# Other places for the weight clamps, both first M in one run, and one batch's state scores moved, in a block-recurrent attention with a gelu MLP behind it

## The chip, the cores and the metric

The kernel runs on one core of a Trainium2 chip. The metric is the time of one execution on the device, in microseconds (us); lower is better. Five runs of the kernel before the change gave a median of 696.96 us.

The engines have short names here: PE is the tensor engine (matmuls; PEld its weight loads), DVE the vector engine, ACT the scalar engine, SP the engine whose queue issues the DMAs. Each engine works through its own instructions in the order in which the kernel emits them. Matmuls write to PSUM, which is used here as eight banks of 128x512 floats.

## The reference

There are two parts. The first is attention between a sequence `x` (8 batches, 8 heads, 512 tokens, 64 wide) and a small state (32 rows per head). The second is a feed-forward layer on the result: 4352 tokens, 512 wide, 2048 hidden, with a gelu in its sigmoid form.

```python
scores = scale * np.matmul(x, state.transpose(0, 1, 3, 2))
a = softmax(scores)                      # over the 32 state rows
xread = np.matmul(a, state)
scores2 = scale * np.matmul(state, x.transpose(0, 1, 3, 2))
a2 = softmax(scores2)                    # over the 512 tokens
sread = np.matmul(a2, x)
out = np.concatenate([xread, sread], axis=2)
...
h = x @ w_in
g = h * (1.0 / (1.0 + np.exp(-1.702 * h)))
return g @ w_out
```

Here `softmax` stands for the lines that subtract the maximum, take the exponential and divide by the sum plus 1e-9. Everything is float32, but the weights `w_in` and `w_out` come as 64-bit floats and are turned into 32-bit floats on the chip.

## The kernel before, in words

**Weights.** The two weight matrices are read in 32 pieces, 16 of `w_in` (four chunks `c` of 512 hidden columns, four row blocks each, so pieces 0 to 3 belong to chunk 0) and 16 of `w_out`. A piece is loaded raw by SP (512 KB, line 199) and then rounded from 64-bit words to float32. The steps of one piece are, on DVE, a mask of the exponent bits (`mask`, line 221), on ACT two Relu passes that clamp the exponent and turn it into a power of two (`round_a`, lines 232 and 233; the pair is called a clamp here), and on DVE again four steps in `fraction` and `round_b`: the mantissa's upper bits (line 239), the sign into the power (line 250), the lower bits (line 253), and the product (line 257). Line 250 needs the clamp. Pieces 18 and 19 are clamped on DVE instead.

`powers_to(n)` emits mask and clamp of all pieces below `n` that have not had them. `round_to(n, ahead)` emits the rounding of all pieces below `n`; within the rounding of piece `i`, after line 250, it asks for the clamps of the pieces up to `i + ahead`, so `ahead` says how far the clamps run in front. `AHEAD` is 3. The masks and powers lie in four buffers, used in turn.

**Attention and the first product.** For batch `b` and chunk `c`, `att_M(b, c)` multiplies the state by the weights of the chunk (M, 8 matmuls in two passes each, line 375), and copies the two results out of PSUM on ACT (line 482). `up_x(b, f)` multiplies M by the transposed attention `aT` (2 matmuls in two passes each, line 553) and applies the gelu on ACT as it leaves PSUM (line 556). So no hidden value of a batch can be made before its M's copy. Batches 0 and 1 run through this by hand, in the order written in the kernel; batches 2 to 7 and the state rows follow through a general path with Strassen products.

The attention of batches 0 and 1 goes in these steps: `xT_chunk` transposes a quarter of x on PE (line 318) and copies it on ACT (line 319); `x_scores` makes its scores (line 325); `head_max`, `head_sub` (lines 338, 342, DVE), `head_exp` (line 346, ACT) and `head_norm` (lines 352 to 358, DVE) make the softmax; `head_back` transposes it into `aT` in two halves (`g`, line 367 on PE, line 368 the copy on ACT). `att_scores(b)` makes the other scores, state by x (line 375 as well), read only much later by `att_s_max` and `att_s_exp`. `keep_warm(n)` emits `n` matmuls of zeros that nobody reads.

**PSUM.** Four banks `bank_o` have fixed names; the last two of them are `held`, which take batch 0's scores first and batch 1's state scores later. Two banks of the pool `psH` rotate under the tag "h" (batch 1's scores, called `apart`, then the `up_x`), and two of the pool `psA` under the tag "att" (transposes and M). A bank can be written again when its last reader is done.

**Down products.** From about 79 us the down product of batch 0 runs in eight pairs (line 1402, `pair`), each after the rounding of two `w_out` pieces and after sums that DVE makes (line 1332). Batch 1's down product is `strassen_two` with `key == 1`: P1 and P2 by `product`, then P5 and others by `strassen_low`, which uses three banks x, y, z (line 696 is its matmul). Its beginning is

```python
product(x, a11, b11, True)
nc.scalar.copy(y, x)
at(1)
product(z, s1, t1, True)
nc.scalar.copy(c22, z)
at(2)
product(y, s2, t2)
```

Right before P5, P2 fills `bank_o[1]`, which is also the `o` that P5 is given, and the line `tt(osb, bank(1), k1)` reads it on DVE (line 752 is that helper).

Of the kernel before, what the change touches and what calls it, by code (L numbers as in the profile page):

```python
# [10 lines left out]
FP32 = mybir.dt.float32  # L11
# [9 lines left out]
def kernel(  # L21
# [30 lines left out]
    nc = tc.nc  # L52

    B, H, S, D = x.shape
# [3 lines left out]
    P = 128  # L58
    NPR = P // Ns
    NG = H // NPR  # L60
    NF = DF // P
    SCH = S // P
    ST = S + Ns
    FC = 512
# [17 lines left out]
    apool = ctx.enter_context(tc.tile_pool(name="apool", bufs=1))  # L82
# [10 lines left out]
    def att_ps(shape, name):  # L93
        return psA.tile(shape, FP32, tag="att", name=name)

    ident = konst.tile([P, P], FP32, name="ident")
# [18 lines left out]
    low = konst.tile([P, 6, S], FP32, name="low")  # L115
# [13 lines left out]
    def keep_warm(n, bank=None):  # L129
        ps = psH.tile([P, FC], FP32, tag="h", name="warm") if bank is None else bank  # L130
        for _ in range(n):
            nc.tensor.matmul(ps, zeros[:, :P], zeros, start=True, stop=True)
# [49 lines left out]
    AHEAD = 3  # L182
# [33 lines left out]
    def mask(i):  # L216

        _, hi = words(i)
        sc = low[:, 2 + i % (AHEAD + 1)].bitcast(I32)
        power[i] = sc  # L220
        nc.vector.tensor_scalar(sc, hi, 0x7FF00000, None, ALU.bitwise_and)  # L221
# [37 lines left out]
    done = {"load": 0, "a": 0, "b": 0, "credit": 0.0}  # L259
# [11 lines left out]
    def powers_to(n):  # L271
        while done["a"] < min(n, len(PIECES)):
            load_weights(done["a"] + 1)
            round_a(done["a"])
            done["a"] += 1

    def round_to(n, ahead=AHEAD):

        nin = NFC * NPR
        while done["b"] < min(n, len(PIECES)):  # L280
            i = done["b"]
            powers_to(i + 1)
            round_b(i, min(i + 1 + ahead, i + 3 if i > nin + 3 else i + 2 if i >= nin else nin), i >= nin or i + 1 < nin and (i + 1 < n or i >= NPR))
            done["b"] += 1
            while done["b"] > NPR and done["load"] < len(PIECES) and before(done["load"]) < done["b"]:
                load_weights(done["load"] + 1)
# [25 lines left out]
    def xT_chunk(b, c):  # L312

        if c == 0:
            A[b]["xT"] = apool.tile([P, NPR, S], FP32, tag="xT", name=f"xT_{b}")
        ps = att_ps([P, NPR, P], f"xT_{b}_{c}")
        for j in range(NPR):
            nc.tensor.transpose(ps[:, j], x_heads(b, c, j), ident)
        nc.scalar.copy(A[b]["xT"][:, :, P * c : P * (c + 1)], ps)

    def x_scores(b, c, banks):

        ps = banks[c // 2].rearrange("p (c g j n) -> p c g j n", c=2, g=NG, j=NPR)[:, c % 2]
        for j in range(NPR):
            nc.tensor.matmul(ps[:, :, j], A[b]["xT"][:, j, P * c : P * (c + 1)], pairs[:, j], start=True, stop=True)
# [22 lines left out]
    def head_norm(b):  # L348

        t = A[b]["e1"]  # L350
        sm = apool.tile([P, NS1], FP32, tag="sm", name=f"sm_{b}")
        nc.vector.reduce_sum(out=sm, in_=t.rearrange("p c g j n -> p (c g j) n"), axis=AX.X)
        nc.vector.tensor_scalar(sm, sm, eps, None, ALU.add)
        nc.vector.reciprocal(out=sm, in_=sm)
        sm = sm.rearrange("p (c g j) -> p c g j", c=SCH, g=NG)
        for g in range(NG):
            e = t[:, :, g]
            nc.vector.tensor_tensor(out=e, in0=e, in1=sm[:, :, g].to_broadcast((P, SCH, NPR, Ns)), op=ALU.mult)

    def head_back(b):  # L360

        a = A[b]
        a["aT"] = low[:, :NG] if b == 1 else apool.tile([P, NG, S], FP32, tag="aT", name=f"aT_{b}")
        for g in range(NG):
            ps = att_ps([P, SCH, P], f"aT_{b}_{g}")
            for c in range(SCH):
                nc.tensor.transpose(ps[:, c], a["e1"][:, c, g].rearrange("p j n -> p (j n)"), ident)
            nc.scalar.copy(a["aT"][:, g], ps.rearrange("p c q -> p (c q)"))

    def by_state(b, ps, rhs):  # L370

# [5 lines left out]
    def att_scores(b):  # L377
        a = A[b]
        a["s"] = bank_o[:NG] if b == 0 else bank_o[NG:]
        by_state(b, a["s"], lambda rows, j: a["xT"][rows, j])  # L380
# [89 lines left out]
    def att_M(b, c, spare=False, banks=None):  # L470

        m = mpool.tile([P, NG, FC], FP32, tag=f"M{turns['M'] % NFC if b < 2 else c}", name=f"M_{b}_{c}")
        turns["M"] += 1
        A[b]["M", c] = m
        name = f"M_{b}_{c}_"
        ps = banks or [
            psH.tile([P, FC], FP32, tag="h", name=name + str(g)) if spare else att_ps([P, FC], name + str(g)) for g in range(NG)
        ]
        by_state(b, ps, lambda rows, j: w_in[c][rows, j])
        for w in (slice(0, P), slice(P, FC)) if (b, c) == (0, 0) else (slice(0, FC),):  # L480
            for g in range(NG):
                nc.scalar.copy(m[:, g, w], ps[g][:, w])  # L482


    squares = dram.tile([SCH, Ns, NG, NPR, P], FP32, name="squares")
# [72 lines left out]
    def up_x(b, f, spare=False, bank=None):  # L558
        c, o = divmod(P * f, FC)
        m = A[b]["M", c]  # L560
        up(b, f, S, [m[:, g, o : o + P] for g in range(NG)], [A[b]["aT"][:, g] for g in range(NG)], spare, bank)

    S1, S2 = (later[:, 4 * i : 4 * i + 4].rearrange("p f n -> p (f n)").rearrange("p (f t) -> p f t", f=HF) for i in range(2))
# [79 lines left out]
    low_a, low_b = ([low[:, 3 * i + k].rearrange("p (f n) -> p f n", f=QF) for k in range(3)] for i in range(2))  # L643
# [44 lines left out]
    def strassen_low(left, right, bank, R, at):  # L688

        b11, t3, b21, b22, t1, t2, t4 = right  # L690
        a11, a12, a21, a22, s1, s2, s4 = left
        x, y, z = (v[:, :P] for v in bank)

        def product(ps, lhs, rhs, first=False):
            for f in range(QF):
                nc.tensor.matmul(  # L696
                    ps, lhs[f], rhs[:, f], start=(first and f == 0), stop=(f == QF - 1), skip_group_check=True
                )

        def add(out, x0, x1):  # L700
            nc.vector.tensor_tensor(out=out, in0=x0, in1=x1, op=ALU.add)

        c11, c12, c21, c22 = (R[:, i, P * k : P * (k + 1)] for i in range(2) for k in range(2))
# [7 lines that stand above are left out]
        nc.scalar.copy(c12, y)  # L711
        at(3)
        product(x, a12, b21)
        nc.scalar.copy(c11, x)
        at(4)
        product(y, a21, t3)
        add(c22, y, c22)
        at(5)
        product(z, s4, b22)
        add(c12, z, c12)  # L720
        at(6)
        product(y, a22, t4)
        nc.scalar.copy(c21, y)
        at(7)

    def strassen_two(key, dst, hooks, a4):

        B11, B21, B22 = w_out[:, :HF, :HN], w_out[:, HF:, :HN], w_out[:, HF:, HN:]
        g = [G[key, u] for u in range(HF)]
# [57 lines left out]
        def left_of(s, *rooms):  # L787
            z = [[s[:, QF * k + f, P * i : P * (i + 1)] for f in range(QF)] for i in range(2) for k in range(2)]
            return *z, *(blocks(v) for v in rooms)
# [42 lines left out]
        else:  # L832

            m = [mpool.tile([P, NG, FC], FP32, tag=f"M{i}", name="spare_M") for i in range(2)]
# [10 lines left out]
            o, h0, h1 = low_banks()  # L845
# [39 lines left out]
            hook(f"P5.{i}")  # L885

        b11, t3, b21, b22 = halves_of(T1)
        strassen_low(left_of(S1, *r), (b11, t3, b21, b22, *low_b), [h0, h1, o], p5, at)
        low_load(6, 1)
        hook("P5")  # L890
        o, h0, h1 = low_banks()
# [335 lines left out]
    mask(3)  # L1227
    xT_chunk(1, 2)
    x_scores(1, 1, apart)
    keep_warm(2, held[0])  # L1230
    xT_chunk(1, 3)
    x_scores(1, 2, apart)
    powers_to(4)
    head_norm(0)
    x_scores(1, 3, apart)
    head_back(0)
    keep_warm(4, held[0])
    round_to(NPR, 0)
    att_M(0, 0)
    powers_to(NPR + 1)  # L1240
    for i in range(2):
        head_max(1, i, apart)
    for i in range(2):
        head_sub(1, i, apart)
    head_exp(1)
    up_x(0, 0, bank=held[0])
    up_x(0, 1, bank=held[1])
    att_M(1, 0)
    round_to(NPR + 1, 0)
    mask(NPR + 1)  # L1250
    mask(NPR + 2)
    head_norm(1)
    up_x(0, 2)
    powers_to(NPR + 2)
    up_x(0, 3)
    att_scores(1)
    head_back(1)
    powers_to(NPR + 3)

    def turn(b, c, then, n=()):  # L1260

        for i in range(nper):
            if i == nper - 1 and then:
                att_M(*then)
            up_x(b, nper * c + i)
            if i < len(n):
                rounds(n[i])

    for i in range(nper):
        up_x(1, i)  # L1270
        if i + 1 < nper:
            round_to(done["b"] + 1, 2)
    att_M(0, 1)
    turn(0, 1, (1, 1), [1, 1, 1])
    round_to(3 * NPR)
    turn(1, 1, (0, 2), [1, 1])
# [310 lines left out]
```

## Time and profile before

| | |
|---|---|
| median of 5 runs | 696.96 us (696.46 to 697.17) |
| the profiled execution | 696.47 us |
| its span in the profile | 694.7 us |
| PE busy | 682.6 us, 98% of the span |
| DVE busy | 560.5 us, 81% |
| ACT busy | 324.3 us, 47% |
| granted PE clock | 0.999 |

The profile is one execution. Its span runs from the first to the last instruction that the profile records; the execution's own time is 1.77 us longer. Busy times are averages over stages that differ: between 37 and 46 us ACT is busy 8.55 of 9 us, between 90 and 130 us 15.53 of 40. A matmul's recorded duration overlaps the next one's, so a row of matmuls is best timed from start to start. "Idle before" an instruction is ascribed to what released it, as the semaphores let one infer.

### The profile page before, as it was taken

To read this page: it belongs to the slowest core of one execution; us is meant where nothing else is said; L and a number is where in the kernel's file an instruction comes from. 1 tells how busy PE (TensorE), PEld (TensorE's weight loads), DVE (VectorE), ACT (ScalarE), POOL (GpSimd) and SP (SyncE) were. 2 spreads that over 40 slices of the span, in tenths; PEclk is the share of its full clock that TensorE was granted. 3 is DMA by queue.
4 is the path that set the end of the run, shared out by engine and by line. 5 is a ranking of instruction groups with operands and counts; after the bars stand their busy time and mean duration, and the time that the engine had idled before them with its cause. 6 is when DMAs were issued, how large, how long until landed. Compare 5 with 4: busy or idle time off the path is not lost.

```text
span 694.7 us, 13670 instructions
## 1 busy us (share of the span) xinstructions
PE 682.6 (98%) x5378; PEld 583.1 (84%) x5378; DVE 560.5 (81%) x1074; ACT 324.3 (47%) x714; POOL 1.0 (0%) x9
## 2 busy tenths in 40 slices
PE   7999999999999999999999999999999999999996
PEld 4533587778998899889988999989988998999995
DVE  5889998999999888788969796988788895886540
ACT  5788844224337523753355435643375236421410
POOL 0000000000000000000000000000000000000000
PEclk9999999999999999999999999999999999999999
DMA  9911337056533564346541755176424740251001
GB/s 237 374 63 61 122 121 167 21 196 189 177 84 119 170 191 143 64 132 189 150 96 48 226 168 117 24 185 202 121 46 138 213 138 16 76 165 46 5 1 30
DMA packets 106320, 87.41 MB, mean 126 GB/s; under 512 B 64784, under 2 KB 85776, under 8 KB 106256
## 3 DMA queue, kind: packets, MB, share of 16 engines
q1 hardware_dynamic: 106256, 86.53, 43.4%
q8 instruction: 43, 0.70, 0.4%
q14 instruction: 21, 0.17, 0.1%
HBM read 68.94 MB, written 17.56 MB: 125 GB/s over the span
## 4 chain that ended last, share of the span: by engine, by line
PE 94%; DMA 2%; ACT 2%; SPq 1%; issue 0%; DVE 0%; DVEq 0%
PE low L696 28%; PE o L1106 15%; PE o L696 15%; PE upx L1106 6%; PE h L553 5%; PE M L375 4%; PE o L1402 4%; PE down L1402 3%; PE o L595 2%; PE upw L1106 2%; PE down_up L553 2%; PE o L745 1%; PE sr L524 1%; PE o L375 1%; PE upx_sr L1106 1%; DMA out_dram<-osb_sr 1%
## 5 line engine op out<-in xcount | busy, mean ns | idle before, releaser
L696 PE MATMUL low<-w_out,g_room 128*128 128x128 f32 x416 | 54.3, 276 | 0.0
L696 PEld LDWEIGHTS low<-w_out,g_room 128*128 128x128 f32 x416 | 50.5, 192 | 4.5 <-issue 4.2
L1106 PE MATMUL o<-ta,M 128*128 128x256 f32 x192 | 49.9, 382 | 0.0
L1106 PE MATMUL upx<-aT,M 128*128 128x256 f32 x192 | 49.3, 379 | 0.0
L696 PE MATMUL low<-low,g_room 128*128 128x128 f32 x336 | 43.3, 275 | 0.0
L1106 PEld LDWEIGHTS o<-ta,M 128*128 128x128 f32 x192 | 35.5, 190 | 5.9 <-ACT g_room L1152 1.6
L696 PEld LDWEIGHTS low<-low,g_room 128*128 128x128 f32 x336 | 40.3, 192 | 0.0
L1106 PEld LDWEIGHTS upx<-aT,M 128*128 128x128 f32 x192 | 36.0, 190 | 4.7
L482 ACT COPY M<-M 128x512 f32<-128x512 f32 (+2 forms) x61 | 30.9, 581 | 17.2 <-PE M L375 17.1
L1112 ACT ACTIVATE g_room<-o 128x512 f32<-128x512 f32 (+1 forms) x56 | 31.3, 560 | 10.4 <-PE o L1106 10.4
L696 PE MATMUL low<-sums,later 128*128 128x128 f32 x280 | 35.8, 275 | 0.0
L696 PEld LDWEIGHTS low<-sums,later 128*128 128x128 f32 x280 | 33.6, 192 | 0.1
L375 PE MATMUL M<-w_in,stT 64*32 64x512 f32 x472 | 33.0, 595 | 0.0
L752 DVE TENSOR_TENSOR g_room<-g_room 128x512 f32<-128x512 f32 x48 | 31.7, 685 | 0.2
L1106 PE MATMUL o<-ta,ms 128*128 128x256 f32 x120 | 30.8, 379 | 0.0
L1152 ACT COPY g_room<-o 128x512 f32<-128x512 f32 (+1 forms) x28 | 15.5, 555 | 25.4 <-PE o L1106 25.4
L1112 ACT ACTIVATE g_room<-g_room 128x512 f32<-128x512 f32 (+1 forms) x28 | 16.8, 600 | 20.8 <-DVE g_room L1115 20.8
L553 PE MATMUL h<-aT,M 128*128 128x512 f32 x56 | 25.3, 600 | 0.8 <-ACT M L482 0.8
L1106 PEld LDWEIGHTS o<-ta,ms 128*128 128x128 f32 x120 | 22.8, 190 | 3.1
L1106 PE MATMUL o<-aT,m 128*128 128x256 f32 x96 | 24.6, 379 | 0.0
L232 ACT ACTIVATE low<-low,edge 128x512 f32<-128x512 int32 x30 | 21.5, 718 | 4.8 <-DVE low L221 4.8
L696 PEld LDWEIGHTS o<-w_out,g_room 128*128 128x128 f32 x160 | 19.4, 192 | 5.0 <-issue 5.0
(293 smaller groups left out, 1627.5 us busy)
## 6 DMA issues: line engine op xcount, KB each, us to landing
low<-low SPq DMA_DIRECT2D x108, 256.0 KB, 2.7
low<-low SPq DMA_DIRECT2D x11, 768.0 KB, 4.4
later<-in_moe_w_out_dram SPq DMA_DIRECT2D x16, 512.0 KB, 3.4
w_out<-in_moe_w_in_dram SPq DMA_DIRECT2D x12, 512.0 KB, 5.2
xsq<-in_x_dram SPq DMA_DIRECT2D x96, 64.0 KB, 2.5
xn<-in_x_dram SPq DMA_DIRECT2D x12, 512.0 KB, 4.3
out_dram<-osb SPq DMA_DIRECT2D x15, 256.0 KB, 2.2
out_dram<-later SPq DMA_DIRECT2D x14, 256.0 KB, 2.1
```

The costliest lines, as they stand in the source:

```text
L232: nc.scalar.activation(out=sc.bitcast(FP32), in_=sc, func=AF.Relu, bias=edge[0], scale=-8.0)
L375: nc.tensor.matmul(ps[g][st], A[b]["stT"][rows, st], rhs(rows, j), start=True, stop=True)
L482: nc.scalar.copy(m[:, g, w], ps[g][:, w])
L524: nc.tensor.matmul(ps[st, g], e, v, start=(c == 0), stop=(c == SCH - 1),)
L553: nc.tensor.matmul(hps, lhs[i], rhs[i], start=(i == 0), stop=(i == n - 1))
L595: nc.tensor.matmul(ps[:, r], lhs[f][:, P * r : P * (r + 1)], rhs[:, f], start=(first and r == 0 and f == 0), stop=(f == HF - 1), skip_grou ...
L696: nc.tensor.matmul(ps, lhs[f], rhs[:, f], start=(first and f == 0), stop=(f == QF - 1), skip_group_check=True)
L752: nc.vector.tensor_tensor(out=out, in0=x0, in1=x1, op=op)
L1106: nc.tensor.matmul(ps[:, k], lhs[i][:, o : o + P], rhs[i], start=(first and k == 0 and i == 0), stop=(i == n - 1), skip_group_check=True,)
L1112: nc.scalar.activation(out=dst, in_=src, func=AF.Gelu_apprx_sigmoid)
L1152: nc.scalar.copy(c12, Y(u))
L1402: nc.tensor.matmul(ps7[name][:, HN * r : HN * (r + 1)], lhs[:, P * r : P * (r + 1)], rhs, start=(i == 0 and r == 0), stop=(i == HF - 1), s ...
```

## The change

The order of the work on batches 0 and 1 between about 19 and 52 us is written differently:

- The clamp of piece 3 is asked for ahead of the last x transposes of batch 1, no longer behind them.
- `head_back` takes its half `g` as an argument. Batch 0's halves stand between the score chunks of batch 1, batch 1's directly behind `up_x(0, 2)`.
- Three warming matmuls instead of four before the first M.
- The clamp of piece 4 is asked for within the rounding of piece 3; masks 5 and 6 come before batch 1's `head_max`.
- M(1, 0) follows M(0, 0) on PE and goes to the held banks; `up_x(0, 0)` and `up_x(0, 1)` go to the att banks instead of the held ones, and `up_x(1, 0)` and `up_x(1, 1)` to the held ones. The clamp of piece 5 stands before `up_x(0, 0)`, that of piece 6 behind the two halves of `head_back(1)`.
- The copies of M(0, 0) are two whole ones, no longer four parts.
- From piece 6 on, `round_to` runs three pieces ahead instead of two, so that the clamps of pieces 9 and 10 come one `up_x` earlier.
- `att_scores(1)` stands behind M(0, 1) instead of before `head_back(1)`.
- In batch 1's P5 the banks y and z are exchanged.

```diff
-    def head_back(b):
+    def head_back(b, g):
...
-        for g in range(NG):
-            ps = att_ps([P, SCH, P], f"aT_{b}_{g}")
...
@@ att_M
-        for w in (slice(0, P), slice(P, FC)) if (b, c) == (0, 0) else (slice(0, FC),):
-            for g in range(NG):
-                nc.scalar.copy(m[:, g, w], ps[g][:, w])
+        for g in range(NG):
+            nc.scalar.copy(m[:, g], ps[g])
@@ strassen_two
-        strassen_low(left_of(S1, *r), (b11, t3, b21, b22, *low_b), [h0, h1, o], p5, at)
+        strassen_low(left_of(S1, *r), (b11, t3, b21, b22, *low_b), [h0, o, h1] if key == 1 else [h0, h1, o], p5, at)
@@ the order written by hand
     x_scores(1, 1, apart)
+    powers_to(4)
     keep_warm(2, held[0])
     xT_chunk(1, 3)
+    head_norm(0)
+    head_back(0, 0)
     x_scores(1, 2, apart)
-    powers_to(4)
-    head_norm(0)
+    head_back(0, 1)
     x_scores(1, 3, apart)
-    head_back(0)
-    keep_warm(4, held[0])
-    round_to(NPR, 0)
+    keep_warm(3, held[0])
+    round_to(NPR, 1)
     att_M(0, 0)
-    powers_to(NPR + 1)
+    mask(NPR + 1)
+    mask(NPR + 2)
     for i in range(2):
         head_max(1, i, apart)
     for i in range(2):
         head_sub(1, i, apart)
     head_exp(1)
-    up_x(0, 0, bank=held[0])
-    up_x(0, 1, bank=held[1])
-    att_M(1, 0)
+    att_M(1, 0, banks=held)
+    powers_to(NPR + 2)
+    up_x(0, 0, True)
+    up_x(0, 1, True)
     round_to(NPR + 1, 0)
-    mask(NPR + 1)
-    mask(NPR + 2)
     head_norm(1)
     up_x(0, 2)
-    powers_to(NPR + 2)
+    for g in range(NG):
+        head_back(1, g)
+    powers_to(NPR + 3)
     up_x(0, 3)
-    att_scores(1)
-    head_back(1)
-    powers_to(NPR + 3)
...
     for i in range(nper):
-        up_x(1, i)
+        up_x(1, i, bank=held[i] if i < 2 else None)
         if i + 1 < nper:
-            round_to(done["b"] + 1, 2)
+            round_to(done["b"] + 1, 2 if i == 0 else AHEAD)
     att_M(0, 1)
+    att_scores(1)
     turn(0, 1, (1, 1), [1, 1, 1])
```

More of the change, by code (lines that the diff above doesn't have):

```diff
@@ L358, in head_norm @@
             nc.vector.tensor_tensor(out=e, in0=e, in1=sm[:, :, g].to_broadcast((P, SCH, NPR, Ns)), op=ALU.mult)
-    def head_back(b):
+    def head_back(b, g):
         a = A[b]
-        a["aT"] = low[:, :NG] if b == 1 else apool.tile([P, NG, S], FP32, tag="aT", name=f"aT_{b}")
-        for g in range(NG):
-            ps = att_ps([P, SCH, P], f"aT_{b}_{g}")
-            for c in range(SCH):
-                nc.tensor.transpose(ps[:, c], a["e1"][:, c, g].rearrange("p j n -> p (j n)"), ident)
-            nc.scalar.copy(a["aT"][:, g], ps.rearrange("p c q -> p (c q)"))
+        if g == 0:
+            a["aT"] = low[:, :NG] if b == 1 else apool.tile([P, NG, S], FP32, tag="aT", name=f"aT_{b}")
+        ps = att_ps([P, SCH, P], f"aT_{b}_{g}")
+        for c in range(SCH):
+            nc.tensor.transpose(ps[:, c], a["e1"][:, c, g].rearrange("p j n -> p (j n)"), ident)
+        nc.scalar.copy(a["aT"][:, g], ps.rearrange("p c q -> p (c q)"))
     def by_state(b, ps, rhs):
```

## The prediction, made before the changed kernel was run

> **What bounds the kernel now.** I read the page's busy shares and its chain first.
>
> ```profile
> PE 682.6 (98%) x5378; PEld 583.1 (84%) x5378; DVE 560.5 (81%) x1074; ACT 324.3 (47%) x714; POOL 1.0 (0%) x9
> ...
> PE 94%; DMA 2%; ACT 2%; SPq 1%; issue 0%; DVE 0%; DVEq 0%
> ```
>
> TensorE (PE) carries 94% of the chain, so an edit saves time only where PE stands still or does work that is not needed. The list of what PE waited for (us in total, times, longest) has these that the diff touches:
>
> ```profile
> PE h L553 <- ACT M L482: 2.0, 2, 1.2
> ...
> PE o L553 <- ACT M L482: 0.3, 1, 0.3
> PE o L696 <- DVE osb L752: 0.3, 1, 0.3
> ```
>
> Line 482 is the copy of an M out of PSUM, line 752 the DVE addition into osb in batch 1. The chain from 17 to 64 us, in order of time (start, us, what), shows how such a wait comes about:
>
> ```profile
> 24.54 1.68 PE M L375 x16
> ...
> 45.44 0.57 ACT M L482
> ...
> 50.68 0.72 ACT low L233
> 51.41 0.49 ACT g_room L556
> 51.89 0.62 ACT low L232
> ...
> 53.74 0.62 ACT low L232
> ...
> 54.38 0.72 ACT low L233
> 55.11 0.48 ACT M L482
> ...
> 55.63 5.42 PE h L553 x12
> ```
>
> Three things are to be seen. M of (batch 0, chunk 0) takes 1.68 us at 24.54, where the others take 1.02: its last quarter waits for piece 3, rounded on DVE until 25.06. At 45.44 PE waits for the copy of M(0,1), which the next matmul needs at once. From 48 to 55.6 the chain runs on ACT: gelu, clamp (L232, L233), gelu, clamp, and M(1,1)'s copy behind them, while PE stands 1.49 us (54.14 to 55.63). The busy time by stretch agrees (PE, PEld, DVE, ACT, POOL; the last numbers are granted clock, DMA share, GB/s):
>
> ```profile
> 25.00:37.00 12.00, 11.56 (x72) 4.23 (x60) 10.81 (x22) 9.72 (x18) 0.00 (x0) 1.00 0.78 313
> 37.00:46.00 9.00, 8.15 (x32) 3.14 (x32) 7.75 (x17) 8.55 (x16) 0.00 (x0) 1.00 0.00 0
> 46.00:56.00 10.00, 8.72 (x33) 3.35 (x34) 9.28 (x20) 8.29 (x16) 0.00 (x0) 1.00 0.55 172
> 56.00:64.00 8.00, 8.00 (x33) 3.13 (x32) 7.96 (x16) 5.87 (x11) 0.00 (x0) 1.00 0.12 47
> ```
>
> PE is idle 0.85 and 1.28 us of the second and third stretch, with ACT at 8.55 of 9 and 8.29 of 10; from 56 us on PE is full.
>
> **Prices.** A clamp costs ACT 1.37 us, a gelu 0.48, start to start:
>
> ```profile
> 49.94 0.71 ACT L232 ACTIVATE low<-low,edge 128x512 f32<-128x512 int32 x1
> 50.68 0.72 ACT L233 ACTIVATE low<-low,edge 128x512 int32<-128x512 f32 x1
> 51.31 0.58 ACT L556 ACTIVATE g_room<-h 128x512 f32<-128x512 f32 x1
> 51.79 0.71 ACT L232 ACTIVATE low<-low,edge 128x512 f32<-128x512 int32 x1
> ```
>
> From further timeline rows. ACT: copy of an M or an aT half 0.47 to 0.48; head_exp and the table load after it
>
> ```profile
> 28.67 1.04 ACT L346 ACTIVATE e<-e 128x1024 f32<-128x1024 f32 x1
> 29.73 1.28 ACT L556 ACT_TABLE_LOAD   x1
> 31.03 1.08 ACT L556 ACTIVATE g_room<-o 128x512 f32<-128x512 f32 x2
> ```
>
> 1.06 and 1.30. PE: an up_x 1.72, its gelu can start 2.02 after its start (37.15 to 39.17); an M 1.02, copies can start 1.20 after its start (60.98 to 62.18) and the next up_x 0.63 after the copy's start (45.42 to 46.05); half a head_back 0.43, its copy 0.69 after its start (35.82, 36.51); a chunk of scores 0.86, a warming matmul 0.215. DVE: first step of a rounding (L250) 0.61, mask and fraction 0.34 each, the other two 0.60.
>
> **The first part, 20 to 37 us.** Up to 20.8 only ACT differs: clamp 3 now stands ahead of the last xT copy, at 19.82, and ends at 21.28, not 23.01. DVE, which sat 1.01 us for it, does L250 of piece 3 at 21.97 instead of 23.04; mask 4 is put in between (the one piece asked for ahead), so piece 3 is done at 24.2, not 25.06. PE: half of head_back at 21.10 (DVE's first product ends 21.05), scores, the other half, scores, three warming matmuls instead of four, M(0,0) from 24.40 to 25.42 without its 0.66 wait, and M(1,0), now into the held banks, to 26.44. The M(0,0) copies in two runs instead of four make the first take 0.58 instead of 0.26, but M(1,0) lies over that: copies at 25.60 and 26.07, up_x(0,0) at 26.5, as before, with 1.02 of M already done. Clamp 4 sits in ACT's gap at 23.55.
>
> Masks 5 and 6 (0.34 each) now stand ahead of head_max, which starts at 24.8 (before 25.32); head_sub ends at 27.27 (27.79). ACT from there: head_exp 27.31, M(1,0) copies 28.37 and 28.84, clamp 5 29.31, table load 30.68, gelus (0,0) to (0,2) at 31.98, 32.46, 32.94. So the change adds a wait: up_x(0,0) and (0,1) now use the att banks, and head_back(1) needs them next. PE is done with up_x(0,2) at 31.75, stands until 32.60 (end of the first gelu, 0.58, plus 0.04), and ends head_back(1) at 33.5; all of PE's queue stands behind it. DVE has those inputs at 32.2 and is not the last. aT copies 33.42 and 33.9, clamp 6 34.37, gelu(0,3) 35.74. On PE up_x(0,3) ends at 35.35 and up_x(1,0) starts, 1.80 before its 37.15; batch 1's state scores (1.02) are still owed, so 0.78 is gained.
>
> A rule of the Trainium skill speaks against this place: ScalarE: Activation LUTs, What ACT_TABLE_LOAD costs, has each switch of set cost a drain beside the load, about 2.66 us in all. The rows here have the gelu 1.30 after the load's start; by the page's figure gelu(0,0) would come 1.36 later and this stage's final gain would be near 0.7 instead of 2.03.
>
> **The second part, 37 to 56 us.** ACT in the new order: gelu(1,0) 37.37, clamp 7, gelu(1,1) 39.22, clamps 8 and 9 (one more than before), gelu(1,2) 42.44, clamp 10, gelu(1,3) 44.29, M(0,1) copies 44.77. PE ends the four up_x at 42.25, M(0,1) at 43.27 and the state scores, now here, at 44.29; up_x(0,4) waits for the copy until 45.40 (before 46.05). So the scores cost nothing here, but the clamps pulled ahead delay the copy by 1.4, and PE stands 1.1. Then one clamp, not two, lies between gelu(0,4) and gelu(0,5): gelu(0,4) 47.42, clamp 11, gelu 49.27, clamp 12, gelu 51.12, clamp 13, M(1,1) copy 52.97, up_x(1,4) at 53.60 instead of 55.63: 2.03 us. PE waits there only 0.4. DVE keeps up: L250 of pieces 6 and 7 wait for their clamps until 35.9 and 39.2, piece 7 is done at 41.8 (M(0,1) needs it at 42.9), piece 15 at 60.7 against 63.8.
>
> What hides the rest: after 56 us the order is unchanged. DVE is 97% busy there, and must stay ahead of PE. Its closest result is the t_room sum ending 86.18 for a matmul at 86.75, 0.57; but DVE enters the stage 3.0 us earlier, PE 2.03. The rounding that waited 2.35 us for a load at 122.08 ends at 126.5, its matmul starts 128.73; that load is queued on SP behind x loads issued as DVE frees the raw pieces, so it moves too, and if it didn't, 2.19 covers 2.03. SP's order is unchanged.
>
> **The third part, batch 1's P5.**
>
> ```profile
> 164.54 1.05 PE L696 MATMUL low<-sums,later 128*128 128x128 f32 x8
> 165.16 0.69 DVE L752 TENSOR_TENSOR osb<-o,g_room 128x512 f32<-128x512 f32 x1 [0.59 <-ACT e L414]
> ...
> 165.90 1.16 PE L696 MATMUL o<-low,spare_M 128*128 128x128 f32 x8 [0.31 <-DVE osb L752]
> ```
>
> PE has the second product ready at 165.43 (164.54 and 8 instructions of 0.89 together) but its bank is the one osb is read from, until 165.85: 0.47 lost. With the two banks swapped the second product goes to h1, free since 162.3; ACT's copy into o takes over the wait, 165.90 to 166.2, and the third product is due at 166.32. So 0.47 goes; what is late next is a DVE sum ending 181.51 for a matmul at 182.09, 0.53. Ends: nothing, if the copy is later by 0.5, and 0.47.
>
> **Sum.** 2.03 + 0.47 = 2.50, off this execution's 696.47 (span 694.7, 1.77 around it): 693.97. The median of the five runs is 0.49 above this execution, so 694.5.
>
> Unknown prices. Masks 5 and 6 need weight pieces that before touched only at 30.0 and 30.95. Piece 4 landed 4.9 us after its issue, at 20.7; the furthest row is 11.3, of a piece issued at 20.88 into a full queue. At the 0.52 MB a piece and 400 GB/s of that stretch, piece 6 lands at 23.3, over 1 us before mask 6: nothing, nearest to the 4.9 row; the other end is rival three. Should head_back's first half wait for both DVE products, PE is 0.64 late at 24, inside its 0.85 wait for the bank.
>
> **Rivals.** One, ACT pays back: the pulled clamps fill ACT's queue without emptying it later, so up_x(1,4) follows up_x(0,4) at the old distance of 9.58. Then only 46.05 - 45.40 = 0.65 stays, plus 0.47: 695.8. For it: ACT is 8.55 of 9 busy. Against: the chain above counts two clamps there and the new order one.
>
> Two, DVE does not follow: if its 3 us are lost on the way (it waits for ACT's exps at 76.8 and for loads), the gain is capped by the 0.57 at 86.75, plus 0.47: 695.9. Against: what it waits for moves with PE.
>
> Three, slower: piece 6 lands by the 11.3 row, at 28.3, and mask 6, ahead of head_max on DVE, holds DVE until then instead of 24.46. The whole ACT chain from head_exp is 3.8 later, and 2.50 saved becomes 1.3 lost: 698.3. It decides from 2.5 us of delay, a landing after 27. Against: the piece issued two before it took 4.9.
>
> That the bank swap only moves the wait is the lower end of part three: 694.9.
>
> **Chances.** Forecast 0.70 (its own range 693.4 to 695.4: 0.7 either way on ACT's chain, whose two new waits of 0.85 and 1.1 can shrink or grow, with 0.35 between runs downward, or with half of P5's 0.47 upward), rivals one and two together 0.20 (695.6 to 696.6), three 0.07, no change for other reasons 0.03. Eight in ten lie from 693.4 to 696.3. A measurement here tells about 0.2%, 1.4 us, from no change: faster by more 0.74 (the forecast and an edge of the rivals), within 0.19, slower 0.07.
>
> **What would show it.** Right: M(0,0) takes 1.02; piece 3's L250 near 22; head_back(1) waits near 0.85 for a gelu; up_x(0,4) waits about 1.1 for M's copy; one clamp between the gelus of up_x(0,4) to (0,6); up_x(1,4) near 53.6; P5's second product 0.89 after the first. Wrong: DVE idle ahead of mask 4, 5 or 6 for a DMA; a gap of 2.7 between table load and gelu; up_x(0,4) later than 46; PE waiting for DVE from 79 to 147.

## The result, and the profile after

| | before | after |
|---|---|---|
| median of the runs on the same chips | 696.68 us (47 runs) | 694.50 us (26 runs) |
| the profiled execution | 696.47 us | 694.47 us |
| its span | 694.7 us | 692.7 us |

After to before is 0.9967, 95% interval 0.9960 to 0.9974: the changed kernel is 2.2 us faster, and the forecast was 694.5. In some executions of these kernels the granted PE clock falls to 0.50 near 20 us and they take some microseconds longer; where runs with a low mean clock weigh on a median, those with 0.998 or more are given beside it.

The page's line of PE and its chain by engine, after:

```profile
PE 682.1 (98%) x5377; PEld 583.3 (84%) x5377; DVE 560.7 (81%) x1074; ACT 324.0 (47%) x712; POOL 1.0 (0%) x9
...
PE 92%; SPq 2%; DMA 2%; ACT 2%; DVE 1%; issue 0%; DVEq 0%
```

PE does the same products and one warming matmul less. It is busy 0.5 us less (the row of M(0,0), which before held a wait for piece 3, is 1.09 long instead of 1.70), and the other 1.5 of the 2 us came out of its idle time. The list of PE's waits after (us in total, times, longest):

```profile
PE aT L367 <- ACT g_room L555: 1.1, 1, 1.1
PE h L552 <- ACT M L481: 1.1, 1, 1.1
```

Before there were two waits for M's copy, 2.0 in all, 0.3 for M(0,0), 0.3 for osb and 0.2 for a copy of aT. After there is one for M's copy, ahead of `up_x(0,4)`, the new one of `head_back(1)` for the bank that the first gelu must free, and 0.2 ahead of `head_back(0)`. The chain from 17 to 62 us (start, us, what) shows the same in order:

```profile
17.42 7.47 DMA w_out<-in_moe_w_in_dram
...
24.92 0.48 DVE low L221
25.40 1.20 DVE mx L338 x2
...
27.82 1.06 ACT e L346
...
31.24 1.28 ACT L555
...
32.53 0.61 ACT g_room L555
...
33.18 1.14 PE aT L367 x8
...
45.31 0.48 ACT M L481
...
45.84 5.42 PE h L552 x12
51.26 1.02 PE M L375 x16
52.28 7.19 PE h L552 x16
```

It begins with a weight load that lands 7.47 us after its issue, on which mask 6 waits at the head of `head_max`. It then goes through the softmax and ACT (head_exp, M(1,0) copies, clamp 5, table load, first gelu). PE has it from 33.18 to 37.8, ACT once more from there to M(0,1)'s copy at 45.31, behind gelus and clamps, and from 45.84 on it stays on PE, where before it came back to ACT until 55.63. The same stretches as before agree (PE, PEld, DVE, ACT, POOL; then clock, DMA share, GB/s):

```profile
25.00:37.00 12.00, 10.90 (x59) 4.75 (x44) 11.23 (x21) 10.46 (x17) 0.00 (x0) 1.00 0.82 329
37.00:46.00 9.00, 7.95 (x47) 2.93 (x46) 8.58 (x19) 8.07 (x14) 0.00 (x0) 1.00 0.09 26
46.00:56.00 10.00, 10.00 (x37) 3.89 (x38) 9.95 (x20) 8.28 (x15) 0.00 (x0) 1.00 0.54 187
```

The first two stretches are emptier on PE than before (10.90 for 11.56, 7.95 for 8.15), the third is full. `up_x(1,4)` starts at 54.05, before at 55.63: 1.58 earlier. At P5 (timeline: start, us, engine, line):

```profile
162.96 1.05 PE L695 MATMUL low<-sums,later 128*128 128x128 f32 x8
163.21 0.69 DVE L751 TENSOR_TENSOR osb<-o,g_room 128x512 f32<-128x512 f32 x1 [0.23 <-PE o L744]
163.85 1.06 PE L695 MATMUL low<-low,spare_M 128*128 128x128 f32 x8
```

The second product follows 0.89 after the first, without the 0.47 of before. But osb also starts 0.25 after the first product, where before it was 0.62, and nothing in the change was meant to do that. From P5's first product to the first of P6, the product group behind it, took 6.83 us before and 6.40 after: 0.43. So 1.58 + 0.43 = 2.01 between the two profiled executions, of the 2.00 that their own times differ.

### The profile page after: what moved, and what is told of

Its sections match the earlier page's. It is cut to its first block, busy times and chain, and to the rows that moved or that the text cites. A ratio compares the mean times of both kernels' runs of the same rounds, so it can differ in the third digit from the quotient of the medians.

```text
span 692.7 us, 13667 instructions
## 1 busy us (share of the span) xinstructions
PE 682.1 (98%) x5377; PEld 583.3 (84%) x5377; DVE 560.7 (81%) x1074; ACT 324.0 (47%) x712; POOL 1.0 (0%) x9
## 4 chain that ended last, share of the span: by engine, by line
PE 92%; SPq 2%; DMA 2%; ACT 2%; DVE 1%; issue 0%; DVEq 0%
PE low L695 28%; PE o L1105 15%; PE o L695 15%; PE upx L1105 6%; PE h L552 4%; PE o L1402 4%; PE M L375 4%; PE down L1402 3%; PE o L594 2%; PE upw L1105 2%; PE o L744 2%; PE down_up L552 2%; SPq L155 1%; PE sr L523 1%; DMA w_out<-in_moe_w_in_dram 1%; PE upx_sr L1105 1%
## 5 line engine op out<-in xcount | busy, mean ns | idle before, releaser
L481 ACT COPY M<-M 128x512 f32<-128x512 f32 x57 | 29.7, 595 | 15.8 <-PE M L375 15.8
L375 PE MATMUL M<-w_in,stT 64*32 64x512 f32 x456 | 31.3, 594 | 0.0
L552 PE MATMUL h<-aT,M 128*128 128x512 f32 x64 | 28.9, 599 | 1.1 <-ACT M L481 1.1
L552 PEld LDWEIGHTS h<-aT,M 128*128 128x128 f32 x64 | 11.8, 190 | 17.4 <-issue 11.5
```

What stands on the lines that cost most here:

```text
L375: nc.tensor.matmul(ps[g][st], A[b]["stT"][rows, st], rhs(rows, j), start=True, stop=True)
L481: nc.scalar.copy(m[:, g], ps[g])
L552: nc.tensor.matmul(hps, lhs[i], rhs[i], start=(i == 0), stop=(i == n - 1))
```

## The experiments

Two theories had to be told apart. Mine: ACT's queue, from batch 1's softmax on, sets PE's times up to `up_x(1,4)`; the parts of the change overlap, and do not add. The rival: each part has its own stall, and the parts add.

### The exchange of banks: undone, and alone

Undone in the changed kernel, made in the kernel before:

```diff
-strassen_low(..., [h0, o, h1] if key == 1 else [h0, h1, o], p5, at)
+strassen_low(..., [h0, h1, o], p5, at)
```

> The changed kernel with the banks of batch 1's P5 as before. Theory (the swap alone is worth what the profile shows at that place, 0.43 us: 0.58 less up to the third product, 0.15 lost again on the sixth): P5's second product comes 1.36 after its first instead of 0.89, all before it is unchanged, the time is 0.4 to 0.5 above the changed kernel's. Rival (PE meets another wait for DVE further on, so the swap is worth nothing): no difference, within 0.15.

> The kernel before with the two banks of batch 1's P5 exchanged, nothing else. The kernel changed but for the swap had P5's second product 1.00 after the first, not 1.36 as the kernel before, and its third 2.00 after it, not 2.36, since DVE's osb began 0.26 and not 0.62 after P5's first product. Theory (the late osb of the kernel before was one execution's, and the swap is worth 0.06 to 0.1): the time is that of the kernel before within 0.15, osb starts about 0.26 after P5's first product. Rival (osb is late in the kernel before as such, and the swap hides it): 0.4 to 0.5 shorter, osb 0.6 after.

Undone: 694.23 us (5 runs), 0.9968 of before (0.9955 to 0.9980), as the changed kernel. P5 to P6 took 6.46 us instead of 6.40; osb started 0.26 after P5's first product. Alone: 696.50 us (11 runs), 1.0001 (0.9990 to 1.0012); 6.76 us instead of 6.83, osb 0.61 after. Neither text had it whole: the time is the theory's, the late osb the rival's. So the exchange is worth 0.06 to 0.07 us, not 0.47. What gives the rest is osb's earlier start, and that came with the other parts.

### The place of one instruction in DVE's stream

osb's sum waits for PE and ACT. In the kernel before, the semaphore wait ahead of it ended at 164.76, 0.04 after PE's signal, ACT's signal was older (in the changed kernel the sum starts at 163.21, ahead of ACT's next signal at 163.27), and the sum still started only at 165.16, 0.40 after its wait instead of 0.04. Counted from 0 over the instructions recorded on DVE, waits included, the sum is number 319 in the kernel before and in the one with the exchange alone, and 317, 318, 320 or 321 in the others, whose queues have one wait more or some fewer. Only at 319 does it pause. Two kernels shift the count, by one small instruction near 77 us: before with one more, after with one less (that one leaves out the addition of 1e-9 to one of the softmax's sums):

```diff
     def s_norm(b, g):                   # before, one more
         e, sm = A[b]["e2"][g]
+        if (b, g) == (0, 0):
+            nc.vector.tensor_scalar(sm, sm, 1.0, None, ALU.mult)
         nc.vector.tensor_scalar(sm, sm, eps, None, ALU.add)
...
     def s_norm(b, g):                   # after, one less
         e, sm = A[b]["e2"][g]
-        nc.vector.tensor_scalar(sm, sm, eps, None, ALU.add)
+        if (b, g) != (0, 0):
+            nc.vector.tensor_scalar(sm, sm, eps, None, ALU.add)
```

> The kernel before with one VectorE instruction more, a 128x1 multiplication by 1 in the column softmax of state 0 near 77 us (row: 0.14 to 0.15 us, where TensorE waits for nothing of VectorE). Theory: the 0.36 us by which VectorE's sum at P5 starts late in the kernel before (0.62 us after P5's first product instead of 0.26) is no wait for data; that sum is VectorE's 319th recorded instruction, directly behind a semaphore wait, and the pause goes with that place in the instruction stream (in the kernel with the second part alone, a pause of the same size stands at instruction 959, which is 5 times 128 further on). One instruction more moves it: the sum starts 0.26 us after P5's first product, P5's start to P6's first product falls from 6.83 to about 6.46 us, and the time falls by 0.3 to 0.4 us from the kernel before. Rival: the pause has to do with data or with transfers, and an instruction more changes nothing there: 0.6 us stays, time unchanged or 0.1 us longer.

> The changed kernel with one VectorE instruction fewer before P5: the addition of 1e-9 to the sums of state 0's first group is left out. Theory: VectorE's sum at P5 becomes the 319th recorded instruction again, directly behind its wait, and starts 0.6 us after P5's first product instead of 0.25; P5's start to P6's first product grows from 6.40 to about 6.76 us, as in the kernel with the exchange of banks alone; time 0.3 to 0.4 us longer than the changed kernel. Rival: nothing changes there (6.40 us), time as the changed kernel's.

DVE's row of osb in the kernel before with one more, and in the changed one with one less, with the PE row that the latter delays:

```profile
165.04 0.69 DVE L754 TENSOR_TENSOR osb<-o,g_room 128x512 f32<-128x512 f32 x1 [0.22 <-PE o L747]
```

```profile
163.15 0.69 DVE L752 TENSOR_TENSOR osb<-o,g_room 128x512 f32<-128x512 f32 x1 [0.59 <-ACT e L414]
...
168.31 1.16 PE L696 MATMUL o<-low,later 128*128 128x128 f32 x8 [0.24 <-DVE spare_M L701]
```

| kernel | osb's number on DVE | osb starts after P5's first product | P5 to P6 |
|---|---|---|---|
| before | 319 | 0.62 us | 6.83 us |
| before, one more | 320 | 0.25 | 6.46 |
| exchange alone | 319 | 0.61 | 6.76 |
| after, exchange undone | 320 | 0.26 | 6.46 |
| after | 320 | 0.25 | 6.40 |
| after, one less | 319 | 0.62 | 6.77 |

In both kernels the count's theory came to within 0.01 us: 6.46 and 6.77 where 6.46 and 6.76 were expected. One more instruction took before from 696.67 (31 runs) to 696.25 us (11 runs): 0.42, though the ratio, 0.9996 (0.9984 to 1.0008), is not told from no change. One less brought the changed kernel to 695.10 us (7 runs, 694.37 to 697.06), against 0.3 to 0.4 more expected; in its profiled execution (694.42 us) batch 1's second quarter of x was there 0.42 earlier than in the changed kernel's, so the two totals can't be compared. What shows the pause are the rows at P5. So 0.37 of the 0.43 at P5 came from a pause that the change moved by accident. The row's "ACT e L414" is a wrong lead: it is the last signal that fits, and it had come 0.31 earlier.

The same pause of 0.35 to 0.37 stands at DVE's number 959 in the kernels with the first part alone, the second alone, and clamps two ahead, again directly behind a wait; there it costs PE about 0.2 us near 495 us. 959 is 319 and five times 128. The traces have a third such place, six times 128 on: number 1087, behind a wait, starts 0.40 after it in five kernels (before, the exchange alone, after with one less, clamps two ahead, the first part alone); the same instruction at another number starts 0.05 after it if it is itself a wait, and at most 0.21 after it if it is an operation. At 575, twice 128 on, the transpose that stands behind a wait in the kernel before starts after 0.11, so not every such place has the pause. The trace has a queue that brings some engine instructions in packets of 8192 bytes, a few times in 100 us. A pause where one block of instructions ends and the next begins, directly behind a wait, fits that. But the packets nearest to the pauses come behind them (with clamps two ahead at 496.5 and 566.5, for pauses that end at 495.46 and 565.76), so that DVE waits for a fetch was not shown.

### The first part alone, the second part alone

The first alone is the changed kernel with the three undone that make up the others: the exchange, the clamps three ahead, and the place of the state scores. The second alone is put into the kernel before:

```diff
-            round_to(done["b"] + 1, 2)
+            round_to(done["b"] + 1, 2 if i == 0 else AHEAD)
     att_M(0, 1)
+    att_scores(1)
...
-    att_scores(1)
     head_back(1)
```

> The kernel before with the second part alone: clamps of pieces 9 and 10 one up_x earlier, and batch 1's state scores behind M(0,1). Theory (ACT's queue sets up_x(1,4); taking the scores out of the way lets head_back(1) and its copies come 0.9 earlier, and the scores then fill the wait for M(0,1)'s copy): up_x(0,4) about where it was, near 46.2, up_x(1,4) near 54.4 instead of 55.63, the time 1.0 to 1.3 shorter than before. Rival (the gain belongs to the first part): within 0.3 of before.

> The changed kernel with the first part alone: P5's banks as before, clamps never more than two ahead, batch 1's state scores ahead of its last transposes as before. Theory (ScalarE's queue from batch 1's softmax on sets TensorE's times up to up_x(1,4), so parts don't add): the second part's 1.5 us alone overlaps with this one; clamps three ahead were worth 0.25 and the place of the scores and the exchange next to nothing, so the first part alone gives about 0.3 us more than the changed kernel, 1.9 us less than the kernel before, up_x(1,4) at 54.3 to 54.6 us, and VectorE's sum at P5 0.26 us after P5's first product. Rival (parts add): the first part is worth what is left of 2.2 after the second's 1.5, so 0.7 us less than the kernel before, up_x(1,4) at 55.0 us or later.

The second alone: 695.22 us (11 runs), 0.9978 (0.9969 to 0.9986), 1.5 less than before; `up_x(1,4)` at 54.56, 1.07 earlier, and 0.37 at P5 from the shifted count. The first alone: median 695.37 (12 runs), with 0.9989 (0.9977 to 1.0000), but seven of those runs had a clock of at least 0.998, with a median of 694.55, as the changed kernel; its profiled execution of 694.55 has

```profile
44.31 5.42 PE L552 MATMUL h<-aT,M 128*128 128x512 f32 x12 [0.75 <-ACT M L481]
...
53.89 1.55 PE L552 MATMUL h<-low,M 128*128 128x512 f32 x3 [1.23 <-ACT M L481]
```

that is, both waits of before, and `up_x(1,4)` all the same at 53.89, 1.74 earlier than before. Part of that is the execution: batch 1's second quarter of x was there 0.36 earlier than in the changed kernel's profile. Counted from where PE takes up that quarter, `up_x(1,4)` comes 1.54 sooner than before with the first part alone, 1.15 with the second alone and 1.74 with both. So the parts do not add. The copies of aT on ACT (before, the second part alone, after) show what they share:

```profile
36.51 1.07 ACT L368 COPY low<-aT 128x512 f32<-128x512 f32 x2 [0.88 <-PE aT L367]
...
35.66 1.06 ACT L368 COPY low<-aT 128x512 f32<-128x512 f32 x2
...
33.98 1.09 ACT L368 COPY low<-aT 128x512 f32<-128x512 f32 x2
```

The second part alone takes away a wait of 0.88 that ACT had at 36.51 for the transposes of aT, which stood behind the state scores on PE. In the changed kernel the same wait is gone, since ACT's queue, now later by the bank's wait, comes to those copies when PE is done. The first part also brings ACT's work forward: ACT is busy 3.00 us from 20 to 25 before and 4.02 after. Which of the first part's edits gives how much was not tested apart.

### Clamps two ahead, and the state scores in their old place

Each undone by itself in the changed kernel:

```diff
-            round_to(done["b"] + 1, 2 if i == 0 else AHEAD)
+            round_to(done["b"] + 1, 2)
```

```diff
     up_x(0, 2)
+    att_scores(1)
     for g in range(NG):
         head_back(1, g)
...
-        up_x(1, i, bank=held[i] if i < 2 else None)
+        up_x(1, i)
...
     att_M(0, 1)
-    att_scores(1)
```

> The changed kernel with the clamps two pieces ahead for pieces 6 and 7 again, not three. Theory (ACT's whole queue up to M(1,1)'s copy sets the start of up_x(1,4), and that queue holds the same clamps either way): M(0,1)'s copy and up_x(0,4) come 1.1 earlier, at 44.7, two clamps lie between the gelus of up_x(0,4) and up_x(0,5) again, and up_x(1,4) starts at 54.3 against 54.05, so the time is 0.25 longer. Rival (the clamps pulled ahead are the gain, 1.37 for one clamp less in that place): up_x(1,4) near 55.4, 1.4 longer.

> The changed kernel with batch 1's state scores ahead of head_back(1) again, and up_x(1,0) and (1,1) in the rotating banks. Theory (ACT's queue sets the pace; PE stands 1.09 at head_back(1) anyway, and the scores' 1.02 fill that hole instead of the one at up_x(0,4)): head_back(1) starts where it did, near 33.2, up_x(0,4) waits 2.1 instead of 1.05, the time is the changed kernel's within 0.2. Rival (the scores behind M(0,1) hide its copy, and that is a part of the gain): 0.75 to 1.0 longer.

> Once more the changed kernel with batch 1's state scores ahead of its last transposes, as they stood in the kernel before, since the first profile of it fell on an execution in which TensorE's granted clock dropped to 0.50 from 20 to 25 us. Theory: time as the changed kernel's within 0.2 us; the wait for M ahead of up_x(0,4) grows by the scores' 0.8 to 0.9 us and up_x(1,4) starts within 0.2 us of where it did. Rival: the scores' place is worth 0.4 us or more, with up_x(1,4) later by as much.

Executions differ in when x and the weights land, so I compare the time from the first gelu's start to `up_x(1,4)`, which does not hold that: 21.52 us in the changed kernel, 21.51 with the exchange undone, 21.76 with clamps two ahead, 21.74 with the first part alone, 21.52 with the scores in their old place. Clamps three ahead are thus worth 0.22 to 0.24 us, and the scores' place nothing: `up_x(0,4)` waits 1.91 us instead of 1.05, 0.86 more, which is about the scores' own time. Clamps two ahead took 694.90 us (9 runs), 0.9970 (0.9961 to 0.9980); in its profile mask 6 waited for its piece:

```profile
25.22 0.43 DVE L221 TENSOR_SCALAR low<-w_out 128x512 int32<-128x512 int32 x1 [0.39 <-DMA w_out<-in_moe_w_in_dram]
```

Scores in the old place: 695.11 (6 runs) and again 696.47 (11 runs), with ratios of 0.9981 (0.9959 to 1.0003) and 0.9998 (0.9987 to 1.0008). Most of that goes with the clock: at 0.998 or more, the runs were 694.16, 694.28, 694.39 and 694.17, 695.50. The first profile (698.95 us) is of an execution with a low clock (windows; PE busy, then the granted clock, DMA share, GB/s):

```profile
15.00:20.00 5.00, 3.55 (x31) 0.87 1.10 247
20.00:25.00 5.00, 4.78 (x23) 0.50 0.99 349
25.00:30.00 5.00, 5.00 (x55) 0.95 1.03 412
```

### Masks out of the way, and a shorter way to the first gelu

Masks 5 and 6 stand ahead of `head_max` in the changed kernel, and so at the head of the chain. Here 5 goes behind `head_sub` and 6 behind `head_norm(1)`:

```diff
     att_M(0, 0)
-    mask(NPR + 1)
-    mask(NPR + 2)
     for i in range(2):
         head_max(1, i, apart)
     for i in range(2):
         head_sub(1, i, apart)
+    mask(NPR + 1)
     head_exp(1)
...
     head_norm(1)
+    mask(NPR + 2)
```

> The changed kernel with mask 5 behind head_sub and mask 6 behind head_norm(1), not ahead of head_max. Theory (the chain from batch 1's softmax through ACT sets PE's time, and the two masks with mask 6's wait for its load add 0.8 to it): head_max starts at 24.45 instead of 25.26, gelu(0,0) at 31.7 instead of 32.53, DVE's product for head_back(1) ends 0.34 earlier and is then about as late as the gelu; up_x(1,4) comes 0.6 to 0.8 earlier, the time is 0.6 to 0.8 shorter than the changed kernel's. Rival (PE's order or DVE sets the pace): within 0.2, since DVE does the same work in all.

693.84 us (5 runs), 0.9957 (0.9945 to 0.9970): 0.66 less than the changed kernel. `head_max` started 6.80 us after PE took up batch 1's second quarter of x, instead of 7.73, and `up_x(1,4)` 35.66 after it instead of 36.52. Next, both masks behind `head_sub`, and on ACT table load and first two gelus directly behind `head_exp`, with the M(1,0) copies and clamp 5 after them:

```diff
...
+    late = []
-    att_M(1, 0, banks=held)
-    powers_to(NPR + 2)
+    att_M(1, 0, banks=held, late=late)
     up_x(0, 0, True)
     up_x(0, 1, True)
-    round_to(NPR + 1, 0)
+    for fn in late:
+        fn()
+    powers_to(NPR + 2)
     head_norm(1)
+    round_to(NPR + 1, 0)
```

and, with that, clamp 10 behind the copies of M(0,1), clamp 13 behind those of M(1,1), and clamp 14 one `up_x` later:

```diff
-            round_to(done["b"] + 1, 2 if i == 0 else AHEAD)
+            round_to(done["b"] + 1, AHEAD if i == 1 else 2)
...
-                rounds(n[i])
+                round_to(done["b"] + n[i], 2 if (b, c, i) == (0, 1, 2) else AHEAD)
...
-    round_to(3 * NPR)
+    round_to(3 * NPR, 2)
```

> The changed kernel with another order around batch 1's softmax: masks 5 and 6 behind head_sub; on ACT the table load and the gelus of up_x(0,0) and (0,1) directly behind head_exp, M(1,0)'s copies and clamp 5 behind them; on DVE head_norm(1) ahead of the rounding of piece 4. Theory (the ACT chain from head_sub to up_x(1,4) sets PE's time): gelu(0,0) near 29.4 instead of 32.5, head_back(1) does not wait, up_x(1,0) starts near 34.6 instead of 35.9, up_x(1,4) near 52.8 instead of 54.05, the time 1.1 to 1.3 shorter than the changed kernel's. Rival (ACT's total work up to M(1,1)'s copy is what counts and the order ahead of it only moves the wait): head_back(1) earlier, but up_x(1,4) within 0.3 of 54.05 and the time within 0.3.

> The order of the kernel before it in this list, and the clamps spread so that none stands right ahead of an M's copy: clamp 10 goes behind M(0,1)'s copy, clamp 13 behind M(1,1)'s and clamp 14 one up_x later. Theory: up_x(0,4) does not wait (near 43.5), up_x(1,4) starts near 51.8, the time is 2.0 to 2.4 shorter than the changed kernel's, 692.3. Rival (the clamps put off are paid later: gelus of up_x(1,4) to (1,6) hold PSUM banks, or DVE gets its clamps too late and w_out's rounding holds PE after 79): 0.5 to 1.3 shorter only.

The first: 693.16 us (6 runs), 0.9957 (0.9945 to 0.9968), 1.34 less than the changed kernel; its profile fell on an execution with the clock's drop (696.04 us), and still shows no wait ahead of `head_back(1)` and 1.02 ahead of `up_x(0,4)`. The second: 692.68 us (5 runs, 692.38 to 693.24), 0.9943 (0.9931 to 0.9955), the fastest of all, 1.8 less than the changed kernel and 4.0 less than before. Its PE rows have no wait for ACT at either place:

```profile
43.95 5.42 PE L556 MATMUL h<-aT,M 128*128 128x512 f32 x12
...
52.16 3.27 PE L556 MATMUL h<-low,M 128*128 128x512 f32 x7
```

It has not quite the 692.3 of the theory. In the profiled execution, the slowest of the five (693.24), PE took up the second quarter of x 0.54 us later than in the changed kernel's, and PE waits 0.15 at 64.10 for a gelu behind a clamp; what keeps the median 0.4 above was not shown. The changed kernel's interval, 0.9960 to 0.9974, overlaps those of the first two kernels of this section and not this one's.

## Why the prediction was right, and where it was not

**The total.** 694.5 against 694.50. That the point came out exactly is luck: two errors cancelled. Between the profiled executions, the sum was 2.50 and 2.00 came. The sum was then carried to a median: 0.49 was added because the execution before was among its fastest, while the profiled one after stood at its own median. The range was right for its reason only in part: ACT's queue did bring `up_x(1,4)` forward, but the 0.43 at P5 came mostly from something else.

**First part, up to the first gelu.** Each thing told to be seen is there: L250 of piece 3 at 22.17 (forecast 21.97), M(1,0) 0.89 behind M(0,0), so M(0,0) no longer waits inside, the bank's wait ahead of `head_back(1)`. The size was off: gelu(0,0) at 32.53, not 31.98, the bank's wait 1.1, not 0.85, `up_x(1,0)` at 35.88, not 35.35. Of these 0.55, 0.20 stood already at L250 (batch 1's second quarter of x was there 0.16 later in this execution), 0.14 is mask 6's wait for its piece, and the other 0.2 lies in steps of 0.04 to 0.08 along DVE and ACT, the largest of them that I wrote 24.8 for a `head_max` that my own durations (24.2 and two masks of 0.34) put at 24.88. Most of it is still there at `up_x(1,4)`: 54.05 instead of 53.60. There PE does not wait at all, where 0.4 was forecast; from 45.84 on its own work fills the time.

**The unknown price.** This step failed. From piece 4's landing at 20.7 and 400 GB/s I put piece 6's at 23.3, "over 1 us before mask 6: nothing". Piece 6 landed 7.5 us after its issue, at 24.9; mask 6 waited 0.14 here and 0.39 in another execution. The other end, 11.3 us and 3.8 us lost (the third rival), did not come. What I did price, 0.34 for each mask ahead of `head_max`, was really on the path: taking them off, with mask 6's wait, gave 0.66 by the medians.

**Second part.** As a difference it is near: one clamp instead of two between gelu(0,4) and gelu(0,5), and 8.21 us instead of 9.58 between `up_x(0,4)` and `up_x(1,4)`. As a cause it is wrong. I counted 0.78 for the first part, and the other 1.25 of 2.03 for the clamps and the scores. The clamp that goes there comes back ahead of M(0,1)'s copy: 1.37 less, 1.15 more, 0.22 in all. The runs show that the first part alone gives all but about 0.2 of it, and that the second is worth over 1 us only where the first is missing. So the first rival was right that the pulled clamps are paid for. It was wrong on the place and the price: they are paid ahead of `up_x(0,4)`, the old distance of 9.58 did not stay, and little was lost, since little of the gain was theirs.

**Third part.** 0.47 forecast, 0.43 measured, for another reason, so the agreement is luck. Of it 0.06 is the exchange; with the banks exchanged, the lost time goes to a later product, which waits for DVE's additions behind osb (0.24 at 168.31 above), not to the sum at 181.51 that I had named as next. 0.37 is the pause in DVE's stream that went away. My reading was that PE waited for osb; the question I did not ask was why osb, whose inputs were there, started 0.4 us late. "That the bank swap only moves the wait" was the right case.

**The second rival, and the page.** PE waits nowhere for DVE between 79 and 147 us. The Trainium skill (ScalarE: Activation LUTs, What ACT_TABLE_LOAD costs) counts a drain beside the load, about 2.66 us for a switch; here the first gelu starts 1.29 us after the start of the load (31.24 to 32.53). The row of before held, and the page's figure was not to be seen in this case.

## What to carry to other kernels

Where one engine's queue sets another's times over a long stretch, follow that queue from its last wait for data on and count what stands in it; an instruction pulled ahead of one wait is paid at the next unless the engine had idle time there, and parts that free the same queue do not add. The orders that helped further brought the first freed bank forward: masks off the head of the chain, then gelus ahead of copies and clamps that nobody waited for yet. And where an instruction starts late although all its inputs are there, do not credit the next edit with it: shift it by one instruction and look again.

## What the runs showed of the hardware

**A pause in the instruction stream.** DVE paused 0.35 to 0.40 us at recorded instructions 319, 959 and 1087, at different operations, where these stood directly behind a wait; at 319 one instruction more in the queue took the pause away and one less brought it back.

**The clock dropped though the gaps were short.** In the first profile with the scores in their old place, PE was busy 1.55 of the 3 us from 15 to 18, in gaps of at most 0.7 us in which it waited for loads, and the granted clock was 0.50 from about 18.7 to 25.5. It fell again from 49.4 to 52.8, behind PE's wait of 1.9 for M(0,1)'s copy; the second profile of that kernel has the same wait and no drop. Other executions had 1.38 to 1.56 busy in that stretch and no drop (the masks moved, the exchange alone, the fastest kernel), and the one with gelus first had 1.75 and a drop from 18.8 to 25.6. The Trainium skill (TensorE: Matmul & The Clock Gate, HAM oscillation — how this bites in real kernels) has the rule that there be no gaps of over about 3.4 us; no gap here was near that, so the rule is not enough to be safe. A mean clock below 0.998 came in 9 of the 11 later runs with the scores in their old place, in 4 of the 26 of the changed kernel, and in 1 of 31 of the kernel before beside the former. The scores' place can't begin the drop at 18.7 us, since the two orders differ only after 31 us; what does was not settled.

**Loads under load.** Piece 4, in the kernel before, landed 4.9 us after its issue; piece 6, two issues on, took 7.5 us in the changed kernel, with the DMA share at 0.99 from 20 to 25 us. One piece's landing is no price for the next one's.
